# A conformer block on one core: the first chunk of attention scored by seven-product quads, with the key sums computed on GpSimd

## The chip, the cores and the metric

The kernel runs on one core of one Trainium2 chip. The core has a matrix engine (PE in the profile; its weight loads are listed as PEld), a vector engine (DVE), a scalar engine (ACT), GpSimd (POOL) and a queue engine for transfers (SP). Each engine works through its own instructions in order and waits on semaphores for the others. The metric is the device time of one execution in microseconds. Three timed runs of the kernel before the change gave 1851.18, 1851.48 and 1852.26 us, so the median is 1851.48 us.

## The reference

The input is x with 2 batches of 4000 tokens of 512 features, in bf16. Cut to what matters here, the block is:

```
x1 = x + 0.5 * (silu(LN(x) @ w_ff1_a) @ w_ff1_b)
h = LN(x1); q, k, v = h @ w_q, h @ w_k, h @ w_v
p = softmax(q k^T / sqrt(512)); x2 = x1 + (p v) @ w_o
x3 = x2 + conv module (pointwise, gate, depthwise 3, norm over all tokens, silu, pointwise)
x4 = x3 + 0.5 * (silu(LN(x3) @ w_ff2_a) @ w_ff2_b); result LN(x4)
```

The attention is full: each of a batch's 4000 tokens looks at all 4000 tokens. In the kernel w_q and w_k are folded into one matrix M, so the scores are (h M) h^T and the keys are the rows h themselves; w_v and w_o are folded in the same way.

## The kernel before

**Chunks.** The tokens are cut into 16 chunks of up to 512, eight for each batch (the last of a batch has 416). First all chunks pass the first feed-forward part, then `attention` (line 2242) runs over the 16 chunks g as chunks of queries, with the convolution of earlier chunks woven in, and then the second feed-forward part follows. Chunk 0 is the first chunk of the first batch, chunk 8 the first of the second batch.

**Scores.** The keys of a batch are 32 tiles of 128 tokens (tiles 0 to 31; tile 31 is short), and attention steps over them as kt = 0 to 31. A plain tile (`scores`, line 1822) takes four matmuls, one for each 128 of the 512 features, with 512 queries as columns; `exp_pair` takes the exponential out of PSUM. Four tiles can instead be taken together as a quad (`score_quad`, line 2185; quad q holds tiles 4q+2 to 4q+5, and there are seven). A quad sees the keys as a 2x2 matrix of blocks (even and odd tile, lower and upper half of the features) and the queries likewise (halves of the features and of the chunk), and uses Winograd's form of Strassen's product: seven block products instead of eight. Each product is four matmuls of 256 columns. A quad has four steps, at kt = 4q+2 to 4q+5, in three PSUM banks c, x and h. Step 0: product 5 into x, ACT copies it to m5; product 1 into c, ACT copies c to h. Step 1: product 6 onto h, DVE writes x = h + m5, product 2 onto c, exponential of c. Step 2: product 7 onto h, DVE writes m5 = h + m5, product 3 onto x, two exponentials. Step 3: product 4 onto h, exponential of h. `half_quad` does the same for tiles 0 and 1.

**Sums ahead of the products.** The products need sums of blocks. Those of the queries (`q_sums`, line 2086) are four operations for a chunk. Those of the keys (`k_sums`, line 2100) are four operations for a quad on 128x512 bf16: s1 = a21 + a22, s2 = s1 - a11 and s4 = a12 - s2 go to a buffer KF, of which there are two (`k_home` says which of them a quad uses), and a21 is overwritten by a11 - a21. `k_here` issues them in two halves and two ticks later stores the buffer to DRAM (`kfd`); the other chunks of the batch load it again (`k_stream`). All these sums run on DVE.

**Which chunks use quads.** Chunk 0 is plain for tiles 0 to 30, since its key sums are only made in its course, for quad q at kt = 4q+6 and 4q+7 (function `forms`, line 2294), after the plain scores of those tiles. All other chunks use quads. Chunk 8 uses them from the start of its batch: its key sums are made for quads 0 and 1 at the end of chunk 7 and for quads 2 to 6 four ticks ahead of each. Plain scores of chunk 0 rotate through banks 0, 1 and 2, the very banks c, x and h of quads.

**The second product.** p v is taken for pairs of tiles, again by seven products (`pv`), into banks 3 to 6 and so on; its sums of exponentials (`pair_sums`) and of values (`v_here`, in chunk 0) run on DVE.

**What sets the order.** The program only lists operations with the buffers that they read and write. A planner (class `Plan`, line 112) gives each a cost and puts them on the engines in the order in which they would come ready: an engine other than PE may take work up to 16 us ahead of where PE stands in the listed order, and PE may reorder within 8 us (line 2942). Its cost of an operation of n elements is 450 + n ns on POOL (line 148) and 150 + 0.52 n ns for a two-operand bf16 operation on DVE. The order that it finds is fixed in the program; at run time each engine's queue is strictly in order. POOL's queue in chunk 0 also holds a one-column memset behind each load of a tile of values (`key_values`, line 2464), which waits for that load. SP's queue holds all transfers of this stage.

Of the kernel before, what the change touches and what calls it, by code (L numbers as in the profile page):

```python
# [19 lines left out]
TCB = -(-T // CHUNK)  # L20
FC = F // 128
NCK = B * TCB
# [6 lines left out]
QUADS = 7  # L29
HC, HD, HF = CHUNK // 2, D // 2, FC // 2  # L30
KT = -(-T // 128)
# [10 lines left out]
def width(c):  # L42

    return CHUNK if c % TCB < TCB - 1 else T - (TCB - 1) * CHUNK
# [515 lines left out]
class Conformer:  # L560
# [1539 lines left out]
    def k_sums(self, g, q, step):  # L2100

        S, n, b = self.S, self.k_home(g, q), g // TCB
        if step == 4:
            self.k_move(g, q, True)
            return
        if q < 0:
            a11, a12, a21, a22 = [self.hh[:, r, e] for r in range(2) for e in range(2)]
            s1, s2, s4 = [self.KF[n][:, m, 0].rearrange("p j k -> p (j k)") for m in range(3)]
            b_x = self.b_hT[0][0:2]
        else:  # L2110
            x = self.hq[:, q]
            b_x = [self.b_hT[kt // TPC][kt % TPC] for kt in self.quad_tiles(q)]
            a11, a12, a21, a22 = [x[:, :, r, e].rearrange("p u j k -> p u (j k)") for r in range(2) for e in range(2)]
            s1, s2, s4 = [self.KF[n][:, m].rearrange("p u j k -> p u (j k)") for m in range(3)]
        b1, b2, b4 = [[c] for c in self.b_KF[n]]
        out, u, v, op, rd, wr = ((s1, a21, a22, ALU.add, [], b1), (s2, s1, a11, ALU.subtract, b1, b2),
                                 (s4, a12, s2, ALU.subtract, b2, b4), (a21, a11, a21, ALU.subtract, [], b_x[1::2]))[step]
        S.op("DVE", lambda e: e.tensor_tensor(out=out, in0=u, in1=v, op=op), reads=rd + b_x, writes=wr)

    @staticmethod  # L2120
    def k_home(g, q):
        return (q + (g % TCB > 0)) % 2 if q >= 0 else 0

    def k_move(self, g, q, away):

# [116 lines left out]
    def attention(self, old, hook, between):  # L2242

        S = self.S
        for g in range(NCK):
            W, plain = width(g), g == 0
            for kt in range(KT):
                if plain:
                    self.ring = [0, 1, 2]
                else:  # L2250
                    self.ring, self.rings["S"] = list(self.ASIDE.get(kt, (0, 1))), 0
                if 0 < g < NCK - 1 and kt < 2:
                    self.query_quad(g + 1, 1 if kt == 0 else 3)
                if plain and kt < KT - 1 or g % TCB < 1 + (g < TCB) and kt < 2 or kt == KT - 2:
                    ps, b_ps = self.scores(g, kt, None if plain else self.bank(kt if kt < 2 else 0))
                    if kt < KT - 2:
                        self.exp_pair(g, kt, ps, b_ps)
                    else:
                        self.act(self.P30[:, 0:W], ps[:, 0:W], AF.Exp, [b_ps], [self.b_P30], scale=SCALE)
                elif not plain and kt < KT - 2:  # L2260
                    S.front(1000)
                    for step in ((0,), (1, 2), (3,))[kt] if kt < 3 and g % TCB > (g < TCB) else ():
                        self.half_quad(g, step)
                    if kt > 1:
                        self.score_quad(g, *divmod(kt - 2, 4))
                    S.front(0)
                if g < NCK - 2:
                    if kt == KT - 1:
                        self.query_quad(g + 2, 0)
                    if 23 <= kt < 27:  # L2270
                        self.query_sums(g + 2, kt - 23)
                if 0 < g < NCK - 1 and kt == 0:
                    self.query_quad(g + 1, 2)
                if g == 0 and 21 <= kt < 25:
                    self.query_weights(kt - 21)
                if g == 0 and kt < 2:
                    self.pop(old // 2 if kt == 0 else old - old // 2)
                if kt == (21 if g == 0 else 24 if g < NCK - 1 else 16):
                    self.tail_scores(g)
                if g:  # L2280
                    self.units_late(g - 1, kt)
                between(g, kt)
                self.units(g, kt)
                self.next_queries(g, kt, 9 if g else 0)
                hook(g, kt)
                self.forms(g, kt)
                self.keys_swap(g, kt)
                self.tick()
# [5 lines left out]
    def forms(self, g, kt):  # L2294

        if g + 1 < NCK and 27 <= kt < 31:
            self.q_sums(g + 1, kt - 27)
        q, r = divmod(kt - 6, 4)
        if g == 0 and 0 <= q < QUADS and r < 2:
            self.k_here(0, q, r)  # L2300
        for at in {1: (26, 27), TCB: (29, 30)}.get(g, ()):
            if kt == at:
                self.k_here(g, -1, kt % 2 == g % TCB)
        q, r = divmod(kt + 2, 4)
        if r < 2:
            if g == TCB and 1 < q < QUADS:
                self.k_here(g, q, r)
            if g == TCB - 1 and q >= QUADS:
                self.k_here(g + 1, q - QUADS, r)
        q, r = divmod(kt + 3, 4)  # L2310
        if r == 0 and q and (g % TCB if q < QUADS else g and (g + 1) % TCB) and (q != QUADS or g % TCB > (g < TCB)):
            self.k_stream(*((g, q) if q < QUADS else (g + 1, q - QUADS - 1)))
        if g == 0 and kt == 30:
            self.k_stream(1, 0)
        if g:
            if kt == 2:
                self.v_stream(g, 1)
            j, r = divmod(kt + 1, 4)
            if r == 0 and 1 < j < GROUPS:
                self.v_stream(g, j)  # L2320
        if kt == KT - 1 and g + 1 < NCK:
            self.v_stream(g + 1, 0)
# [612 lines left out]
    def program(self, any_score):  # L2935
        i = self.i
        self.any_score = any_score
        S = self.S
# [89 lines left out]
        for dc in range(DC):  # L3028
            self.q_group(0, 0, dc)
            if not any_score:  # L3030
                self.tick()
        if not any_score:
            for n in (0, 1, 2, 3, 4):
                self.v_here(0, n)
        self.pop(1)
# [182 lines left out]
        for k in range(2):  # L3218
# [3 lines left out]
            for ti in pair:  # L3222
# [3 lines left out]
                                                            in1=self.neghalf[0:TILE, two], op=ALU.pow),  # L3226
                 reads=self.b_mv[sl][two] + [self.b_neghalf], writes=self.b_rs[sl][two])
            S.op("DVE", lambda e, two=two: e.scalar_tensor_tensor(
                out=self.sh[sl][:, two], in0=self.mv[sl][:, two, 0], scalar=-1.0, in1=self.rs[sl][:, two],
# [8 lines left out]
        for h in range(2):  # L3238
            for f, (ps, b_ps) in enumerate(self.early):
                out = ps[:, h * HC:(h + 1) * HC].rearrange("p (t k) -> p t k", t=2)  # L3240
# [116 lines left out]
```

## Time and profile before

| what | value |
|---|---|
| median of three runs | 1851.48 us (1851.18 to 1852.26) |
| the profiled execution | 1851.06 us, span of its instructions 1846.9 us |
| granted PE clock | 1.000 |
| busy share of the span | PE 99%, PEld 82%, DVE 81%, ACT 74%, POOL 8% |
| chunk 0 of attention | about 402 to 458 us of the span |
| chunk 8 of attention | about 870 to 932 us of the span |

The profile was taken on a run that is 0.42 us below the median. Its span runs from the first to the last instruction. A row of grouped instructions has the engine, the operation, the regions written and read (out<-in), the shape, the count, then the busy time in us and the mean duration of one in ns, then the idle time of the engine ahead of them and who ended it. The regions are large: "keys" holds key tiles and values, "sums" the exponentials and their sums, "xt" the residual stream and in attention the KF, query-sum and m5 buffers, "work" queries and outputs, "wff" weights and convolution buffers; "s" and "y" are the PSUM banks 0 to 3 and 4 to 7. A row of the timeline has start, length, engine, operation and count, where equal neighbours are merged. A row of a window has its length and for each engine the busy time and the count of instructions.

### The profile page before, as it was taken

The numbers are of one execution on the slowest core, as the hardware profiler recorded it, in microseconds if no ns is written. First come the engines' busy times: TensorE is split into PE (matmuls) and PEld (weight loads), VectorE is DVE, ScalarE is ACT, GpSimd is POOL, SyncE is SP. The second block draws the span as 40 slices with busy tenths as digits, with TensorE's granted clock in tenths as the row PEclk, the third lists the DMA queues.
The fourth block names the chain that finished last, engine by engine and source line by source line (L and its number), as shares of the span: only waits on it lengthen the run. The fifth ranks groups of instructions, "written<-read, shape, count | busy, mean of one in ns | idle before, by whom it ended". The sixth has DMA issues, their size and how long they took to land.

```text
span 1846.9 us, 40836 instructions
## 1 busy us (share of the span) xinstructions
PE 1827.6 (99%) x16082; PEld 1518.8 (82%) x16168; DVE 1491.3 (81%) x3240; ACT 1364.9 (74%) x2433; POOL 144.3 (8%) x357
## 2 busy tenths in 40 slices
PE   9999999999999999999999999999999999999998
PEld 6888888866888888889878888888876888888887
DVE  8889898868766877677876777777779989889886
ACT  6887777755656877787777877887768788777775
POOL 2000000000000000000100000000011000000010
PEclk9999999999999999999999999999999999999999
DMA  7332344287645655458954444543476222211211
GB/s 200 87 91 85 83 111 100 70 245 226 173 144 143 189 153 157 125 151 178 241 146 136 123 116 117 146 122 111 124 218 171 56 69 77 73 47 48 64 44 45
DMA packets 317722, 231.09 MB, mean 125 GB/s; under 512 B 191362, under 2 KB 288325, under 8 KB 317268
## 3 DMA queue, kind: packets, MB, share of 16 engines
q1 hardware_dynamic: 316996, 228.15, 45.7%
q8 instruction: 129, 2.11, 0.5%
q14 instruction: 69, 0.57, 0.1%
q10 hardware_dynamic: 528, 0.26, 0.0%
HBM read 131.15 MB, written 56.22 MB: 101 GB/s over the span
## 4 chain that ended last, share of the span: by engine, by line
PE 95%; DVE 2%; ACT 1%; DMA 1%; issue 1%; SPq 0%; DVEq 0%; ACTq 0%
PE y L95 50%; PE s L95 45%; DVE work L95 1%; ACT work L95 0%; DVE wff L95 0%; ACT sums L95 0%; DMA work<-work 0%; DMA pqd<-wff 0%; ACT keys L95 0%; DVE xt L95 0%; DVE sums L95 0%; DVE s L95 0%; DMA xt<-kfd 0%; DVE keys L95 0%; ACT xt L95 0%
## 5 line engine op out<-in xcount | busy, mean ns | idle before, releaser
L95 ACT ACTIVATE sums<-s 128x512 bf16<-128x512 f32 (+4 forms) x498 | 291.3, 586 | 145.9 <-PE s L95 143.0
L95 ACT ACTIVATE keys<-s 128x512 bf16<-128x512 f32 (+3 forms) x275 | 156.9, 574 | 132.7 <-PE s L95 101.6
L95 DVE TENSOR_TENSOR sums<-sums 128x512 bf16<-128x512 bf16 (+3 forms) x528 | 201.3, 399 | 54.6 <-ACT sums L95 42.2
L95 PE MATMUL y<-work,keys 128*128 128x256 bf16 x1920 | 244.4, 273 | 0.0
L95 PE MATMUL s<-sums 128*128 128x256 bf16 (+1 forms) x1428 | 212.6, 272 | 0.1
L95 PE MATMUL y<-sums,keys 128*128 128x256 bf16 (+1 forms) x1440 | 210.6, 270 | 0.0
L95 PE MATMUL y<-wff,keys 128*128 128x256 bf16 (+2 forms) x1590 | 209.4, 276 | 0.1
L95 ACT ACTIVATE work<-xt,work 128x512 bf16<-128x512 bf16 x260 | 199.5, 784 | 9.5 <-DVE work L95 7.8
L95 PEld LDWEIGHTS y<-work,keys 128*128 128x128 bf16 x1920 | 187.8, 98 | 22.4
L95 PE MATMUL y<-work,wff 128*128 128x256 bf16 (+3 forms) x1324 | 197.2, 272 | 0.1
L95 DVE TENSOR_TENSOR keys<-keys 128x1024 bf16<-128x1024 bf16 (+2 forms) x264 | 170.7, 660 | 22.9 <-ACT keys L95 20.2
L95 PE MATMUL s<-work,keys 128*128 128x256 bf16 (+4 forms) x1329 | 184.6, 275 | 1.0
L95 PEld LDWEIGHTS y<-wff,keys 128*128 128x128 bf16 (+1 forms) x1592 | 151.4, 98 | 30.2 <-issue 3.4
L95 DVE BATCH_NORM_STATS2 work<-xt 128x6 f32<-128x512 bf16 x251 | 164.3, 681 | 2.4 <-DMA xt<-in_x_dram 1.7
L95 PEld LDWEIGHTS s<-sums 128*128 128x128 bf16 x1428 | 139.0, 98 | 22.5 <-DVE s L95 0.4
L95 PEld LDWEIGHTS y<-sums,keys 128*128 128x128 bf16 x1440 | 138.1, 98 | 21.3 <-issue 2.9
L95 POOL TENSOR_TENSOR work<-work 128x4 f32<-128x4 f32 (+3 forms) x108 | 91.2, 845 | 764.8 <-DVE work L95 741.8
L95 PE MATMUL s<-xt,keys 128*128 128x256 bf16 (+1 forms) x924 | 142.3, 270 | 1.2 <-DVE s L95 1.1
L95 PEld LDWEIGHTS y<-work,wff 128*128 128x128 bf16 x1324 | 127.3, 98 | 17.6 <-DVE wff L95 0.4
L95 PE MATMUL y<-sums,xt 128*128 128x256 bf16 (+1 forms) x960 | 140.7, 270 | 0.3 <-DVE sums L95 0.3
L95 PEld LDWEIGHTS s<-work,keys 128*128 128x128 bf16 (+1 forms) x1348 | 107.7, 97 | 34.9 <-ACT sums L95 2.2
L95 PE MATMUL s<-xt 128*128 128x256 bf16 (+1 forms) x893 | 131.4, 270 | 1.3 <-DMA xt<-kfd 0.9
(163 smaller groups left out, 3343.9 us busy)
## 6 DMA issues: line engine op xcount, KB each, us to landing
xt<-kfd SPq DMA_DIRECT2D x98, 384.0 KB, 3.2
xt<-v12d SPq DMA_DIRECT2D x105, 256.0 KB, 3.1
xd<-xt SPq DMA_DIRECT2D x28, 512.0 KB, 2.7
xt<-xd SPq DMA_DIRECT2D x28, 512.0 KB, 3.8
out_dram<-xt SPq DMA_DIRECT2D x14, 512.0 KB, 2.9
xt<-in_x_dram SPq DMA_DIRECT2D x13, 512.0 KB, 4.4
dcvd<-wff SPq DMA_DIRECT2D x48, 128.0 KB, 2.9
keys<-dcvd SPq DMA_DIRECT2D x12, 512.0 KB, 3.7
```

The source lines that it names most:

```text
L95: return getattr(eng, self.name)(*self.args, **self.kw)
```

## The change

Chunk 0 is plain only for kt below 6 and for tile 30. Its tiles 6 to 29 are scored as quads 1 to 6. For that, `q_sums` of chunk 0 (four operations on DVE) are issued right after its queries, and the key sums of quads 1 to 6 are issued ahead of the quads: of quad 1 at kt = 0 and 1, of quad 2 at 3 and 4, of quad q from 3 to 6 at 4q-3 and 4q-2. Quad 0's key sums follow at kt = 25 and 26, in the other of the two KF buffers than before, in which chunk 1 finds them without a load; the load at kt = 30 is gone. The scores of the short last tile move from kt = 21 to 24 in chunk 0, and scores in chunk 0 from kt = 6 take the banks that they take in other chunks (this also holds for the four groups of chunk 1's queries at kt = 16, 17 and 20). All key sums, of both batches and also those of tiles 0 and 1, are issued on POOL instead of DVE.

```diff
@@ k_sums
-        S.op("DVE", lambda e: e.tensor_tensor(out=out, in0=u, in1=v, op=op), reads=rd + b_x, writes=wr)
+        S.op("POOL", lambda e: e.tensor_tensor(out=out, in0=u, in1=v, op=op), reads=rd + b_x, writes=wr)
@@ k_home
-        return (q + (g % TCB > 0)) % 2 if q >= 0 else 0
+        return (q + (g % TCB > 0 or g + q == 0)) % 2 if q >= 0 else 0
@@ attention
-            W, plain = width(g), g == 0
+            W = width(g)
             for kt in range(KT):
+                plain = g == 0 and kt < 6
...
-                if plain and kt < KT - 1 or g % TCB < 1 + (g < TCB) and kt < 2 or kt == KT - 2:
+                if plain or g % TCB < 1 + (g < TCB) and kt < 2 or kt == KT - 2:
...
-                if kt == (21 if g == 0 else 24 if g < NCK - 1 else 16):
+                if kt == (24 if g < NCK - 1 else 16):
                     self.tail_scores(g)
@@ forms
-        q, r = divmod(kt - 6, 4)
-        if g == 0 and 0 <= q < QUADS and r < 2:
-            self.k_here(0, q, r)
+        if g == 0:
+            q, r = (1, kt) if kt < 2 else (2, kt - 3) if kt < 7 else divmod(kt + 3, 4)
+            if 0 <= r < 2 and q <= QUADS:
+                self.k_here(0, q % QUADS, r)
...
-        if g == 0 and kt == 30:
-            self.k_stream(1, 0)
@@ program
         if not any_score:
+            for n in range(4):
+                self.q_sums(0, n)
             for n in (0, 1, 2, 3, 4):
                 self.v_here(0, n)
```

## The prediction

> **What bounds the kernel now.** I read the page's busy shares first, then its chain that ended last, then windows over the two stretches that the change touches, with the neighbours of chunk 0 as a measure.
>
> ```profile
> span 1846.9 us, 40836 instructions
> PE 1827.6 (99%) x16082; PEld 1518.8 (82%) x16168; DVE 1491.3 (81%) x3240; ACT 1364.9 (74%) x2433; POOL 144.3 (8%) x357
> PE 95%; DVE 2%; ACT 1%; DMA 1%; issue 1%; SPq 0%; DVEq 0%; ACTq 0%
> core 0: us, PE busy (x) PEld busy (x) DVE busy (x) ACT busy (x) POOL busy (x), PEclk, DMA share, GB/s
> 402.00:458.00 56.00, 55.74 (x347) 32.92 (x351) 37.41 (x101) 29.98 (x50) 3.28 (x26) 1.00 0.79 246
> 458.00:518.00 60.00, 59.79 (x534) 49.20 (x538) 43.81 (x103) 37.92 (x71) 2.54 (x9) 1.00 0.66 173
> 518.00:580.00 62.00, 61.08 (x552) 51.43 (x555) 43.48 (x102) 39.69 (x76) 2.70 (x12) 1.00 0.55 152
> 870.00:932.00 62.00, 60.91 (x562) 51.02 (x564) 53.86 (x130) 48.41 (x90) 4.63 (x15) 1.00 0.98 235
> ```
>
> PE is busy for 99% of the span, PE is 95% of the chain, and the clock is full. In chunk 0 (402 to 458 us) PE idles 0.26 us in 56. The end is therefore set by how many columns PE streams. A saved column is saved time, and anything that lets PE wait is lost time. In chunk 8 (870 to 932), which already works by quads with their key sums on DVE, DVE is busy 53.86 of 62 us (87%), and PE idles 1.09 us: that is what quads cost beside a crowded DVE.
>
> **The change part by part. Columns of PE.** Busy time can't price a matmul, since neighbours overlap, so I take runs of equal matmuls in the timeline, and the mean of one from the groups by shape.
>
> ```profile
> 411.93 5.34 PE L95 MATMUL s<-work,keys 128*128 128x512 bf16 x24
> 585.08 1.25 PE L95 MATMUL y<-sums,keys 128*128 128x256 bf16 x10
> 586.83 1.04 PE L95 MATMUL s<-work,xt 128*128 128x256 bf16 x8
> L95 PE MATMUL s<-work,keys 128*128 128x512 bf16 x173 | 43.5, 379 | 1.0
> L95 PE MATMUL s<-work,xt 128*128 128x256 bf16 x438 | 65.0, 273 | 0.0
> ```
>
> A run of n lasts n-1 steps and one full matmul. With 512 columns the step is (5.34 - 0.379) / 23 = 0.2157 us; with 256 columns (1.25 - 0.273) / 9 = 0.1086 and (1.04 - 0.273) / 7 = 0.1096, so 0.109. Four plain tiles are 16 x 0.2157 = 3.451 us, a quad is 28 x 0.109 = 3.052. Six quads save 6 x 0.399 = 2.4 us. The weight loads grow from 16 to 28 for four tiles; chunks that are all quads have PEld at 82% (49.20 of 60) with PE full, so that costs nothing.
>
> **What the quads add on ACT and DVE, and what DVE loses.**
>
> ```profile
> L95 ACT ACTIVATE s<-s 128x512 f32<-128x512 f32 x103 | 60.3, 585 | 19.4 <-PE s L95 16.6 <-PE y L95 2.0
> L95 ACT ACTIVATE xt<-s 128x512 f32<-128x512 f32 x103 | 61.2, 595 | 28.8 <-PE s L95 27.7
> L95 ACT ACTIVATE sums<-s 128x512 bf16<-128x512 f32 x329 | 195.6, 596 | 127.2 <-PE s L95 125.6
> L95 DVE TENSOR_TENSOR s<-s,xt 128x512 f32<-128x512 f32 x103 | 71.9, 698 | 53.3 <-PE s L95 47.8 <-ACT xt L95 3.9 <-PE y L95 0.2
> L95 DVE TENSOR_TENSOR xt<-s,xt 128x512 f32<-128x512 f32 x91 | 62.5, 686 | 26.4 <-PE s L95 26.3
> L95 DVE TENSOR_TENSOR xt<-xt,keys 128x512 bf16<-128x512 bf16 x14 | 5.9, 420 | 0.3
> L95 POOL TENSOR_TENSOR wff<-wff 128x512 bf16<-128x512 bf16 x2 | 2.3, 1156 | 9.5 <-ACT wff L95 9.5
> ```
>
> The exponentials stay as many (four for four tiles, 128x512 each, 0.60 us). ACT gets two copies for each quad, 12 x 0.59 = 7.1 us, and stands at 29.98 + 7.1 = 37 of some 54 us. DVE gets two additions for each quad, 6 x (0.698 + 0.686) = 8.3 us, and four query sums, 4 x 0.42 = 1.7. It loses 28 key sums (7 quads x 4; the row x14 is s2 alone, 7 quads of 2 batches), 28 x 0.42 = 11.8. That leaves 37.41 + 8.3 + 1.7 - 11.8 = 35.6 us. POOL gets 28 x 1.156 = 32.4 us in chunk 0. In chunks 7 and 8 DVE loses 11.8 us and POOL gets the same 32.4; the few sums of tiles 0 and 1 are half as wide, four for each batch, and go with them.
>
> **GpSimd beside DVE.** POOL has so far almost nothing to do in attention, so what it takes from DVE has to be read elsewhere. Early in the program four GpSimd operations on 128x512 run beside DVE:
>
> ```profile
> 23.91 1.28 DVE L95 TENSOR_TENSOR work<-wff 128x1024 bf16<-128x1024 bf16 x2
> 24.75 7.60 POOL L95 TENSOR_SCALAR keys<-keys,work 128x512 bf16<-128x512 bf16 x4
> 25.23 1.79 DVE L95 TENSOR_TENSOR work<-work,wff 128x1024 bf16<-128x1024 bf16 x2
> 28.47 1.78 DVE L95 TENSOR_TENSOR keys<-keys 128x1024 bf16<-128x1024 bf16 x2
> 30.51 1.24 DVE L95 TENSOR_TENSOR sums<-sums,wff 128x512 bf16<-128x512 bf16 x2
> 31.67 0.68 DVE L95 TENSOR_TENSOR sums<-s,sums 128x512 f32<-128x512 f32 x1
> ...
> 1380.38 1.16 POOL L95 TENSOR_TENSOR wff<-wff 128x512 bf16<-128x512 bf16 x1
> 1380.68 1.05 DVE L95 TENSOR_SCALAR work<-xt,work 128x512 bf16<-128x512 bf16 x1
> L95 DVE TENSOR_SCALAR work<-xt,work 128x512 bf16<-128x512 bf16 x18 | 7.2, 437 | 0.1
> ```
>
> Two DVE operations that take 1.28 us alone take 1.79 and 1.78 beside POOL, and two of 0.42 take 1.24: 0.51 + 0.50 + 0.40 = 1.4 us over four POOL operations, 0.35 for each. The nearest row of POOL's own two-operand form held another kind of DVE operation for 1.05 - 0.44 = 0.61 us. So the bounds for one key sum on POOL are 0 (DVE is just then at an addition that reads PSUM, as the 0.68 at 31.67, which is not longer) and 1.156 (DVE stands for all of it). I take 0.35, since those rows are DVE's two-operand sums, what it does most here. Then DVE in chunk 0 is at 35.6 + 28 x 0.35 = 45.4 of 53.6 us, 85%, and in chunk 8 at 53.86 - 11.8 + 9.8 = 51.9 of 62, 84%: relieved there by 2 us only. Beside a DVE at 87% PE idled 1.09 us in chunk 8, so I give chunk 0 after the change 0.9 us of PE idle where it has 0.26: 0.65 us lost. For chunk 8 I take no change, with bounds of -1.1 us (its idle goes) and +1.1 (it doubles).
>
> The Trainium skill, in "SBUF — State Buffer", section "Who interferes with whom", says that a DVE instruction with two SBUF inputs contends with a GpSimd instruction that reads SBUF, and that the later of the two stands still until the first is through. The trace agrees that they hold each other up, but by 0.35 us for a POOL operation of 1.9, not by all of it. By the page's rule the sum would turn to the first rival below.
>
> **The queues.** POOL's longest key sums depend on one another (s1, s2, s4), so a quad takes about 4 x 1.2 to 1.5 = 5 to 6 us there. Six quads fill the time after the plain tiles, some 37 us (the plain run in the timeline ends at 411.93 + 5.34 = 417.3, chunk 0 would end near 455), 6.2 us for each. A KF buffer is free again after product 3, two thirds through its quad, and is needed filled one quad and a third later, some 8 us. So POOL keeps up, with 2 us to spare, and the planner, which counts 962 ns for such an operation where the trace has 1156, is off by less than that. The sums of quads 1 and 2 depend on nothing late and may go up to 16 us ahead. What they can get behind on POOL is this:
>
> ```profile
> POOL keys L95 <- DMA keys<-keysd: 20.1, 18, 6.3
> PE s L95 <- DMA xt<-kfd: 0.9, 1, 0.9
> L95 POOL MEMSET keys<- 128x1 bf16 x24 | 2.2, 100 | 21.9 <-DMA keys<-keysd 20.1 <-DMA keys<-tailsd 1.8
> ```
>
> In chunk 0 POOL waits 18 times for a load of values, up to 6.3 us; a key sum listed behind such a memset waits too, and with it its quad. In turn the memsets now come up to 1.2 us later behind a sum; the values of tiles 15 and up are used ten ticks later, so that is hidden. On SP, the stores of KF wait for POOL where they waited for DVE, and loads queue behind them. One load of 384 KB (quad 0 for chunk 1) goes. I cost these at nothing, with the memsets as the case in which the cover is gone (rival 3). The moved tail scores and the query groups in banks 0 and 1 lie between quads and add no column.
>
> **Sum.** -2.4 (columns) + 0.65 (idle in chunk 0) + 0 (chunk 8) = -1.7 us. Against the profiled execution that is 1851.06 - 1.7 = 1849.4; the median of the runs is 0.42 above it, so 1849.8 us.
>
> **The rivals.**
> 1. *Slower: POOL and DVE shut each other out.* If each of the 28 POOL sums excludes DVE's two-operand sums for its full length, it holds one up by half of it on the mean, 0.58 us. DVE then needs 35.6 + 16.2 = 51.8 us, and with the 87% that chunk 8 shows as workable chunk 0 lasts 59.5 us instead of 56: 1851.5 + 3.5 = 1855. If chunk 8 suffers too (53.86 - 11.8 + 16.2 = 58.3, at 87% 67 us instead of 62), 1860. For it: the 0.61 us under POOL's two-operand form. Against it: the four sums at 24.75 cost 0.35 each. It decides from about 0.55 us for each sum.
> 2. *The chain of a quad sets the pace.* Bank h passes from copy to product 6, addition, product 7, addition, product 4 and exponential before the next quad may copy into it: 0.59 + 0.6 + 0.70 + 0.6 + 0.69 + 0.6 + 0.6 = 4.4 us (a product is three steps of 0.109 and one matmul of 0.273), with some 0.07 at each of seven hand-overs 4.9. In other chunks 62 / 8 = 7.75 us are there for four tiles, here 6.2. If queueing on ACT and DVE adds 2 us, six quads take 41.4 instead of 37.2: +4.2 - 2.4 = +1.8, so 1853.3.
> 3. *The sums come late.* One quad held for the 6.3 us of the longest load wait gives -2.4 + 6.3 = +3.9, so 1855.4. Against it: the planner may place sums of quads 1 and 2 16 us ahead of that wait.
> 4. *More than the columns.* If chunk 8's 1.09 us of idle also goes and chunk 0 gets none, -2.4 - 1.1 = -3.5; with a further stall gone by a new order (0.9 for the load of KF is the longest kind beside) 1847.2.
>
> **How the numbers follow.** A measurement of this kernel can tell about 0.2%, 3.7 us, from no change, so below 1847.8 is faster and above 1855.2 slower. Chances: the forecast (1848.2 to 1850.9) 0.58; rival 1 0.14; rival 2 0.15 (1851 to 1855); rival 3 0.04; rival 4 0.09. Faster is most of rival 4, 0.07; slower is rival 1 and part of 2 and 3, 0.17; within it 0.76. The likeliest is 1849.8. The range from 1847.6 to 1854.6 leaves out the bottom of rival 4 (some 0.05) and rival 1 with most of rival 3 (some 0.15).
>
> **What would show it.** Plain groups of 512 columns in chunk 0 fall from 120 matmuls by 96, and 168 of 256 columns come. POOL shows 56 operations of 128x512, near 1.16 to 1.5 us. DVE's two-operand sums in chunk 0 have a tail of 0.75 to 0.9 us. PE's idle in chunk 0 stays under 1.5 us, and the stretch to the end of chunk 0 is about 1.7 us shorter. I am wrong if PE waits there for "DVE s" or "DVE sums" by several us, if PE waits for POOL at all, or if another stage moves by more than 1 us through a new order.

## The result and the profile after

The changed kernel takes 1874.95 us (median of four runs, 1873.42 to 1878.26) against 1851.87 us for the kernel before on the same chip (four runs, 1851.18 to 1853.21): a ratio of 1.0125, 95% interval 1.0112 to 1.0137. It is slower by 23 us. The forecast was 1849.8 us, and the time lies above the range and above the price of every rival.

The profiled execution of the changed kernel took 1873.42 us. Its page begins with the busy shares, and the chain's first row follows:

```profile
span 1869.5 us, 41150 instructions
PE 1833.9 (98%) x16240; PEld 1524.4 (82%) x16240; DVE 1514.0 (81%) x3192; ACT 1372.4 (73%) x2445; POOL 218.4 (12%) x421
PE 91%; DVE 5%; DMA 2%; ACT 1%; issue 1%; SPq 0%; POOL 0%; DVEq 0%; POOLq 0%; ACTq 0%
```

PE's part of the chain falls from 95% to 91% and DVE's rises from 2% to 5%. One number is odd: DVE has 48 instructions fewer than before (3192 for 3240), since the key sums are gone from it, and yet it is busy for 22.7 us more (1514.0 for 1491.3).

The windows of the changed kernel over the stretches that the prediction used for chunks 0 and 8 show where the time goes (same columns as there):

```profile
402.00:458.00 56.00, 46.40 (x344) 30.80 (x343) 45.74 (x85) 30.71 (x52) 25.54 (x47) 1.00 0.77 223
870.00:932.00 62.00, 57.96 (x558) 48.81 (x556) 50.99 (x101) 45.94 (x89) 28.43 (x33) 1.00 0.89 202
```

In 56 us of chunk 0 PE idles 9.6 us where it idled 0.26. DVE is busy for 45.74 us, almost the 45.4 that was forecast, but it got through only 85 instructions, 0.54 us each, where it had 101 of 0.37 us. It is not that DVE has more to do: it does less in more time.

A stage's place can be compared between kernels by when the first ACT copy of a chunk's second-product result (sums<-y) starts. Against the kernel before, this copy is late by the following, in the profiled executions (one each, good to 1 or 2 us; "all sums on DVE" and "second batch alone" are experiments told below; the profiled execution of "all sums on DVE" is the fastest of its ten, 3.2 us under their median, so its column is low):

| at this copy of | changed kernel | all sums on DVE | second batch alone on GpSimd |
|---|---|---|---|
| chunk 2 | +13.5 | +0.8 | +0.7 |
| chunk 6 | +15.7 | +2.1 | +1.3 |
| chunk 9 | +23.3 | +2.3 | +9.5 |
| end of the span | +22.6 | +0.9 | +9.5 |

The loss is made in two places, some 13 us in and right behind chunk 0 and some 7 to 8 us about chunk 8: the two stretches in which GpSimd makes key sums. The largest of PE's waits over the whole changed kernel (engine, line waited for: us in total, times, longest):

```profile
PE s L95 <- DVE s L95: 7.4, 8, 1.4
PE y L95 <- DVE xt L95: 5.5, 2, 3.2
PE s L95 <- DVE sums L95: 4.6, 3, 1.9
```

In the kernel before, the same view has

```profile
PE s L95 <- DVE s L95: 1.1, 2, 0.8
PE y L95 <- DVE xt L95: 0.9, 1, 0.9
PE s L95 <- DVE sums L95: 0.5, 1, 0.5
```

PE waits for DVE and, in the whole trace, not once for POOL. So the key sums are in time (rival 3 is out), and something makes DVE late. The timeline of the changed kernel shows what. First a quad in chunk 0, then the longest stall, at its end (the rows of DVE and GpSimd, and in the last row PE):

```profile
422.15 0.68 DVE L95 TENSOR_TENSOR xt<-s,xt 128x512 f32<-128x512 f32 x1
422.39 1.16 POOL L95 TENSOR_TENSOR xt<-keys,xt 128x512 bf16<-128x512 bf16 x1 [0.78 <-PE s L95]
422.75 1.08 DVE L95 TENSOR_TENSOR xt<-keys,xt 128x512 bf16<-128x512 bf16 x1
423.63 1.22 POOL L95 TENSOR_TENSOR keys<-keys 128x512 bf16<-128x512 bf16 x1
423.87 1.26 DVE L95 TENSOR_TENSOR keys<-keys 128x512 bf16<-128x512 bf16 x1
...
458.03 1.42 POOL L95 TENSOR_TENSOR xt<-xt,keys 128x512 bf16<-128x512 bf16 x1
458.36 4.29 DVE L95 TENSOR_TENSOR sums<-sums 128x512 bf16<-128x512 bf16 x4
459.58 1.16 POOL L95 TENSOR_TENSOR xt<-keys,xt 128x512 bf16<-128x512 bf16 x1
460.82 1.21 POOL L95 TENSOR_TENSOR keys<-keys 128x512 bf16<-128x512 bf16 x1
462.57 0.41 DVE L95 TENSOR_TENSOR xt<-work 128x512 bf16<-128x512 bf16 x1
462.91 0.41 DVE L95 TENSOR_TENSOR xt<-keys 128x512 bf16<-128x512 bf16 x1
463.35 0.43 DVE L95 TENSOR_TENSOR xt<-keys,xt 128x512 bf16<-128x512 bf16 x1
...
463.83 1.03 PE L95 MATMUL y<-sums,xt 128*128 128x256 bf16 x4 [3.24 <-DVE xt L95]
```

In the kernel before, four such sums in a row read

```profile
416.28 1.68 DVE L95 TENSOR_TENSOR sums<-sums 128x512 bf16<-128x512 bf16 x4 [0.27 <-ACT sums L95]
```

A two-operand sum on DVE that meets a key sum on GpSimd takes 1.26 us instead of 0.42 and ends about when GpSimd's ends (423.87 + 1.26 = 425.13, beside 423.63 + 1.22 = 424.85). The trace gives starts and ends alone, so whether DVE stands or only crawls meanwhile is not told apart. Four in a row beside three key sums take 4.29 us instead of 1.68. What DVE has behind them, here a sum of values that PE needs for the second product, comes later, and PE stands for 3.24 us. The addition at 422.15, which reads PSUM and one operand of SBUF, takes its usual 0.68 us beside a key sum.

### The profile page after: what moved, and what is told of

It is laid out like the page before. It is cut to its first block, busy times and chain, and to the rows that moved or that the text cites. A ratio compares the mean times of both kernels' runs of the same rounds, so it can differ in the third digit from the quotient of the medians.

```text
span 1869.5 us, 41150 instructions
## 1 busy us (share of the span) xinstructions
PE 1833.9 (98%) x16240; PEld 1524.4 (82%) x16240; DVE 1514.0 (81%) x3192; ACT 1372.4 (73%) x2445; POOL 218.4 (12%) x421
## 4 chain that ended last, share of the span: by engine, by line
PE 91%; DVE 5%; DMA 2%; ACT 1%; issue 1%; SPq 0%; POOL 0%; DVEq 0%; POOLq 0%; ACTq 0%
PE y L95 49%; PE s L95 42%; DVE sums L95 2%; DVE work L95 1%; DVE xt L95 1%; DVE wff L95 0%; ACT work L95 0%; DMA dcvd<-wff 0%; DMA work<-work 0%; ACT sums L95 0%; DMA wff<-in_w_ff_a_dram 0%; DVE s L95 0%; DMA xt<-v12d 0%; DMA wff<-keysd 0%; DVE keys L95 0%
## 5 line engine op out<-in xcount | busy, mean ns | idle before, releaser
L95 DVE TENSOR_TENSOR sums<-sums 128x512 bf16<-128x512 bf16 (+3 forms) x528 | 221.0, 436 | 56.4 <-ACT sums L95 44.2
L95 PE MATMUL y<-wff,keys 128*128 128x256 bf16 (+3 forms) x1592 | 210.0, 276 | 0.0
L95 DVE TENSOR_TENSOR keys<-keys 128x1024 bf16<-128x1024 bf16 (+2 forms) x248 | 166.4, 685 | 23.0 <-ACT keys L95 20.2
L95 PE MATMUL s<-work,keys 128*128 128x256 bf16 (+4 forms) x1300 | 172.4, 269 | 4.1 <-DVE xt L95 2.4
L95 PEld LDWEIGHTS s<-sums 128*128 128x128 bf16 x1428 | 139.0, 98 | 22.6 <-DVE s L95 0.4
L95 PE MATMUL s<-xt,keys 128*128 128x256 bf16 (+1 forms) x972 | 149.9, 271 | 7.6 <-DVE s L95 7.4
L95 PE MATMUL s<-xt 128*128 128x256 bf16 (+1 forms) x941 | 138.6, 270 | 1.4 <-ACT s L95 1.1
L95 DVE TENSOR_TENSOR s<-s,xt 128x512 f32<-128x512 f32 (+1 forms) x125 | 85.6, 685 | 63.5 <-PE s L95 52.7
```

What stands on the lines that cost most here:

```text
L95: return getattr(eng, self.name)(*self.args, **self.kw)
```

## The experiments

Theory A: while GpSimd makes a two-operand sum, DVE's two-operand sums on SBUF stand still; DVE works strictly in order, so the whole queue behind is late, and PE with it. Theory B: the quads are too tight a chain for chunk 0 (rival 2). Theory C: the key sums or the order that the planner finds are at fault, not the engine; the texts on record call the planner's part of it Theory D. Each ratio below is against the kernel before on the same chip.

### The key sums back on DVE, the quads kept

```diff
@@ k_sums (the changed kernel)
-        S.op("POOL", lambda e: e.tensor_tensor(...
+        S.op("DVE", lambda e: e.tensor_tensor(...
-        WEIGHTS, TOKENS, TAPS = (14, 16, 18, 20), (24, 25, 26, 27), (8, 11, 14, 17)
+        WEIGHTS, TOKENS, TAPS = (27, 28, 29, 30), (24, 25, 26, 27), (8, 11, 14, 17)
```

The second edit makes the convolution's weight sums later, behind the key norm that reads the same memory; the third run of this list shows what it does alone.

> The changed kernel with all key sums back on DVE (the four sums of the convolution's weights are listed at kt = 27 to 30 instead of 14 to 20, so that they stay behind the norm that still reads the same memory). Theory A, exclusion: while POOL works on a two-operand sum no two-operand sum of DVE starts, and that is the whole loss. Then the loss goes: DVE in chunk 0 is at about 47 of 54 us, PE idles about 1 us there, 1849 to 1853 us. Theory B, the quads of chunk 0 follow one another too tightly (their chain of copies and additions sets the pace): 1862 to 1868 us, with chunk 0 as long as in the changed kernel and only chunk 8 better.

Measured: 1855.18 us (ten runs), ratio 1.0013 (1.0003 to 1.0022). That is above the 1849 to 1853 us expected by theory A and far below theory B's 1862 to 1868. The window and PE's waits of 402 to 458 us:

```profile
402.00:458.00 56.00, 52.75 (x403) 36.84 (x405) 42.18 (x109) 36.19 (x62) 4.04 (x30) 1.00 0.85 245
...
PE s L95 <- ACT s L95: 1.3, 2, 0.8
PE y L95 <- DVE xt L95: 0.8, 1, 0.8
PE s L95 <- DVE s L95: 0.4, 1, 0.4
```

With the key sums back, DVE does 109 instructions in 42.18 us, and 21 of the 23 us are gone. So the loss needs the key sums on GpSimd, and the quads alone do not make it. But the quads bring nothing either: PE now idles 3.25 us in chunk 0, in waits of under 1 us each for ACT's copies (1.3 us), for a sum of values by DVE (0.8) and for DVE's additions (0.4), and that eats the 2.4 us of saved columns. The stalls lie at 435 to 452 us, while quads 1 to 3 (415 to 431 us) run without one.

### The key sums on GpSimd, without quads in chunk 0

```diff
@@ k_sums (the kernel before)
-        S.op("DVE", lambda e: e.tensor_tensor(...
+        S.op("POOL", lambda e: e.tensor_tensor(...
```

> The kernel before with all key sums on POOL and nothing else changed: chunk 0 stays plain. Theory A: DVE's two-operand sums beside POOL's take up to 1.26 us instead of 0.42 in both batches; chunk 8 loses its 6 us as in the changed kernel, chunk 0 loses less than 14 since no quad waits for DVE there: 1858 to 1866 us. Theory B: chunk 0 has no quads, so nothing is lost there, and chunk 8 loses at most what late sums cost: 1851 to 1854 us.

Measured: 1868.64 us (four runs, 1866.99 to 1871.18), ratio 1.0078 (1.0061 to 1.0095).

```profile
402.00:458.00 56.00, 50.86 (x290) 27.34 (x294) 40.23 (x65) 26.91 (x45) 32.04 (x52) 0.97 0.73 226
```

Chunk 0 has no chain of a quad here, and still PE idles 5.1 us in these 56, while DVE does 65 instructions in 40.23 us, 0.62 each. At chunk 2's copy this kernel is 11.8 us late, the changed kernel 13.5. Theory B can't be the cause of that.

The profile is of the slowest of the four executions, 2.5 us above their median. By the medians the size does depend on the quads: without them in chunk 0, the key sums on GpSimd cost 0.78%, with them 1.17% (1.013 of the next run less the 1.0013 above), and the difference of some 7 us is larger than the intervals allow for noise. So about two thirds of the loss need no quad in chunk 0. That the tighter chain of a quad makes the same hold dearer would fit the rest, and no run here shows it. Theory A had expected 1858 to 1866 us, and the time is above that too.

### The changed kernel with the weight sums late

The second edit of the first experiment alone.

> The changed kernel with the four sums of the convolution's weights listed at kt = 27 to 30, the second difference that the run with all sums on DVE had. Both theories: this does not matter, 1873 to 1878 us as the changed kernel. If it gained more than 5 us, part of what was put down to POOL would belong to these sums.

Measured: 1876.45 us (two runs), ratio 1.013 (1.011 to 1.0151), where the changed kernel has 1.0125. The edit does not explain what the key sums on DVE gave back.

### Idle sums on GpSimd that nobody waits for

In the kernel before, GpSimd adds two constant tiles into a tile that nobody reads at that time, once for each key tile of the first 26 of chunk 0. No key sum and no quad is touched, and DVE and ACT run the same operations in the same order as before.

```diff
+                if g == 0 and 0 <= kt < 26:
+                    out = self.QF[3].rearrange("p j k -> p (j k)")
+                    S.op("POOL", lambda e: e.tensor_tensor(out=out, in0=self.Wvo[:, 0, :], in1=self.Wvo[:, 1, :], op=ALU.add), ...
```

> The kernel before with 26 more operations on POOL in chunk 0, one for each kt, that add two 128x512 bf16 pieces of a weight into memory that nobody reads: no one waits for them. Theory A: some 20 of DVE's two-operand sums grow to 0.8 to 1.26 us, DVE's busy time in chunk 0 grows by 8 to 15 us, and the time by 2 to 8 us although nothing depends on POOL. Theory B, and the theory that the sums come too late: no change, 1851 to 1853 us, and DVE's sums stay at 0.42.

Measured: 1859.98 us (seven runs), ratio 1.0036 (1.0025 to 1.0047). First the busy shares of the page (DVE had 1491.3 us for the same 3240 instructions before), then the window, then lines of the timeline:

```profile
PE 1831.8 (99%) x16082; PEld 1519.3 (82%) x16168; DVE 1510.8 (81%) x3240; ACT 1364.6 (73%) x2433; POOL 175.1 (9%) x383
402.00:458.00 56.00, 50.52 (x289) 27.32 (x293) 48.61 (x94) 27.08 (x45) 28.75 (x50) 0.97 0.73 224
...
436.42 3.00 DVE L95 TENSOR_TENSOR sums<-sums 128x512 bf16<-128x512 bf16 x3
436.56 2.58 POOL L95 TENSOR_TENSOR xt<-work 128x512 bf16<-128x512 bf16 x2
438.18 0.61 PE L95 MATMUL s<-sums,keys 128*128 128x256 bf16 x4 [1.58 <-DVE sums L95]
```

Work that no one needs costs 6.7 us (0.36%). DVE's busy time over the whole span rises by 19.5 us (1510.8 - 1491.3) for the same instructions, which is 0.75 us for each of the 26 idle sums. In the window alone it rises by 11.2 us (48.61 - 37.41), but only 21 of the 26 lie in it, and DVE gets seven instructions less done there. Three sums of 0.42 us take 3.00 us beside two on GpSimd. This is theory A by itself: the engines' meeting, not the lateness of anything GpSimd makes, and not a new order.

### The same with copies: one operand read

```diff
+                    S.op("POOL", lambda e: e.tensor_copy(out, self.Wvo[:, 0, :]), ...
```

> As the run with 26 idle two-operand operations, but with copies on POOL, which read one operand. If each operation of POOL that reads shuts DVE's two-operand sums out for its whole length, they grow by up to the length of the copy; if it is the second operand of POOL that collides, they stay near 0.42 to 0.8 and the time near 1852 us.

Measured: 1852.7 us (eight runs), ratio 0.9999 (0.9989 to 1.001). The busy shares, the group of the copies, the window, and two lines of the timeline:

```profile
PE 1826.7 (99%) x16082; PEld 1518.9 (82%) x16168; DVE 1496.9 (81%) x3240; ACT 1365.9 (74%) x2433; POOL 162.4 (9%) x383
L95 POOL COPY xt<-work 128x512 bf16<-128x512 bf16 x26 | 18.2, 700 | 0.8
402.00:458.00 56.00, 55.72 (x348) 32.85 (x352) 41.86 (x104) 31.08 (x53) 15.17 (x48) 1.00 0.81 248
403.57 0.69 POOL L95 COPY xt<-work 128x512 bf16<-128x512 bf16 x1
403.82 0.71 DVE L95 TENSOR_TENSOR xt<-keys,xt 128x512 bf16<-128x512 bf16 x1
```

A sum on DVE that meets a copy takes 0.71 instead of 0.42 us. DVE's busy time rises by 5.6 us over the span (1496.9 - 1491.3), 0.22 for each copy, and the time does not move: PE idles 0.28 us in the window, where it idled 0.26.

### The same with writes: no operand read

Two constants written (memset) for each of the 26 tiles, 52 in all.

```diff
+                    for _ in range(2):
+                        S.op("POOL", lambda e: e.memset(out, 0.0), ...
```

> The kernel before with 52 writes of a constant by GpSimd (128x512, bf16) into a tile that nobody reads at that time, two for each key tile of the first 26 of chunk 0. It asks whether it is reading that holds VectorE off. If only operands that are read count: VectorE's two-operand sums beside them stay at 0.42 us each, its busy time from 402 to 458 us stays at about 37.4 us, and the time is that of before, 1852 to 1854 us. If a write holds it off as well: busy time up by 0.1 us or more for each, 5 us or more in all, and the time 1 to 5 us above that of before, as with e3.

Measured: 1852.4 us (eight runs) against 1851.62, ratio 1.0002 (0.9992 to 1.0013). The busy shares, the group, the window, and two lines of the timeline:

```profile
PE 1831.8 (99%) x16168; PEld 1519.8 (82%) x16168; DVE 1492.6 (81%) x3240; ACT 1365.1 (74%) x2433; POOL 170.1 (9%) x409
L95 POOL MEMSET xt<- 128x512 bf16 x52 | 27.2, 524 | 2.2
402.00:458.00 56.00, 56.00 (x354) 33.12 (x353) 37.44 (x101) 29.88 (x50) 20.66 (x62) 1.00 0.80 249
427.74 1.22 DVE L95 TENSOR_TENSOR sums<-sums 128x512 bf16<-128x512 bf16 x3
427.84 2.85 POOL L95 MEMSET xt<- 128x512 bf16 x5
```

GpSimd is busy for 20.66 us of the window, and DVE's 101 instructions take 37.44 us, as before (37.41); over the span DVE's busy time is 1.3 us up for 52 writes. Three sums beside five writes take 1.22 us, 0.41 each. Here and with the copies, too, DVE and ACT keep the order of the kernel before. So it is what GpSimd reads that holds DVE's sums off.

### A quarter of the sums on GpSimd

In the changed kernel only the fourth sum of each four (a11 - a21, on which no other sum of its quad waits) stays on GpSimd; the weight sums are late.

```diff
-        S.op("POOL", lambda e: e.tensor_tensor(...
+        S.op("POOL" if step == 3 else "DVE", lambda e: e.tensor_tensor(...
```

> The changed kernel with one sum of four on POOL (a21, which no other sum waits for) and three on DVE; convolution weights late. Theory A, exclusion for the length of each POOL sum: a quarter of the POOL sums, so a quarter of the 20 us between the changed kernel and the one with all sums on DVE, ratio 1.003 to 1.005, and DVE's sums that meet one still take up to 1.26 us. Theory C, the loss comes from the three dependent sums s1, s2, s4 being late on POOL: they are on DVE here, so the ratio is that of all sums on DVE, 1.001.

Measured: 1860.61 us (four runs), ratio 1.0047 (1.0031 to 1.0064). Above the kernel with all sums on DVE (1.0013) that is 0.34%, for a quarter of the sums, where all of them cost 1.17% (1.013 less 1.0013). A quarter of that would be 0.29%, so within the intervals a quarter of the sums, spread over both batches, makes a quarter of the loss, and it does so without the chain of dependent sums, which is on DVE here. The loss does not go by the count alone: the next run has twice as many sums on GpSimd, all in the second batch, and loses no more.

### Key sums of the second batch alone on GpSimd

```diff
-        S.op("POOL", lambda e: e.tensor_tensor(...
+        S.op("DVE" if g < TCB else "POOL", lambda e: e.tensor_tensor(...
```

> The changed kernel, its key sums of the first batch (chunk 0) by VectorE, those of the second batch (chunk 8) by GpSimd, and the convolution's weight sums late as in e1. Exclusion (a two-operand sum on GpSimd holds off VectorE's two-operand sums while it runs): chunk 0 goes as in e1 and loses nothing, chunk 8 loses the 6 to 7 us that the joins of the changed kernel show for it; time 1859 to 1863 us against about 1853 before, a ratio of 1.003 to 1.006. If the loss needs the quads' chains as well as GpSimd's sums (a sum that comes late for a chain that cannot wait), chunk 8 is as in the changed kernel too, since its quads are the same in both; if on the other hand chunk 8's loss is only chunk 0's carried on, the time is that of e1, 1854 to 1856 us.

Measured: 1860.61 us (four runs, 1859.75 to 1862.45) against 1851.62, ratio 1.0048 (1.0031 to 1.0064).

```profile
402.00:458.00 56.00, 52.97 (x408) 36.91 (x407) 42.27 (x108) 36.32 (x62) 4.12 (x30) 1.00 0.85 250
870.00:932.00 62.00, 55.85 (x509) 46.02 (x508) 50.11 (x95) 42.38 (x80) 32.98 (x38) 0.98 0.95 219
```

Chunk 0 is that of the kernel with all sums on DVE (52.97 for 52.75 of PE). Chunk 8, which was already made of quads in the kernel before, loses: PE idles 6.2 us where it idled 1.09. Above the kernel with all sums on DVE the time is 0.35%, 6.5 us; from chunk 6 to chunk 9 the table of single profiles has 7.6 us for the changed kernel and 8.2 for this one. The second batch loses on its own, and the first batch is left with the larger part.

### The planner's price of a key sum

The planner counts 962 ns for such an operation on GpSimd. Here it counts 1500.

```diff
-            return 1000 if call.name == "tensor_tensor" and n < 8 else 450 + n
+            return 1000 if call.name == "tensor_tensor" and n < 8 else 1500 if call.name == "tensor_tensor" and n == 512 else 450 + n
```

> The changed kernel with the planner's price for a 512-element two-operand operation on POOL set to 1500 ns instead of 962, so that it lists engines' work for POOL sums as slow as the trace shows or slower. Theory D, the plan is wrong about POOL's speed and all engines run in an order made for faster sums: at least half of the loss goes, 1853 to 1863 us. Theory A: the planner still does not know that DVE stands still, 1868 to 1880 us.

Measured: 1879.52 us (two runs), ratio 1.0147 (1.0127 to 1.0167): no better than the changed kernel. An order that knows GpSimd to be slow does not help, since the plan still doesn't know that DVE stands meanwhile. This part of theory C falls; an order that keeps DVE's sums and GpSimd's apart was not tried.

### The queries of chunk 1 ahead

The stalls that the quads leave on DVE lie among the four groups of chunk 1's queries, which since the change take the banks that other chunks use. Here, with all sums on DVE, they come at kt = 6 in a row.

```diff
-            plan = {14: (0,), 16: (1,), 18: (2,), 20: (3,)} if self.any_score else {16: (0,), 17: (1, 2), 20: (3,)}
+            plan = {14: (0,), 16: (1,), 18: (2,), 20: (3,)} if self.any_score else {6: (0, 1, 2, 3)}
```

> Quads in chunk 0 with all sums on DVE, and chunk 1's four query groups listed at kt = 6 in banks 3, 5 and 7, which are empty until then, instead of at 16, 17 and 20 in banks 0 and 1, which the quads use. Theory B for what is left of the loss (the quads' banks and chain): PE's idle of 3 us in chunk 0 falls under 1.5, and the time falls by 1.5 to 3 us against the run with query groups in banks 0 and 1, to a little below the kernel before (ratio 0.998 to 1.000). If the rest was DVE's load (42 of 56 us), nothing changes: ratio 1.001.

Measured: 1853.74 us (ten runs), ratio 1.0006 (0.9997 to 1.0016).

```profile
402.00:458.00 56.00, 53.17 (x409) 37.28 (x411) 42.06 (x108) 34.62 (x60) 3.65 (x26) 1.00 0.88 244
```

PE's idle in chunk 0 goes from 3.25 to 2.83 us, and the stalls move to 417 to 419 and 438 to 442 us. That the query groups cause them is not borne out. This is the best of the kernels with the quads, and it can't be told from the kernel before.

## Why the prediction was wrong

**The columns.** The matmuls changed as foretold (the count of weight loads rises by 72, from 16168 to 16240, which is 168 - 96), and nothing contradicts the 2.4 us. But they were not time. With the key sums on DVE the quads make the kernel 0.13% (0.03 to 0.22%) slower, 2.4 us, where columns and idle were to give -1.7. The idle of chunk 0 was taken as 0.9 us and is 3.25, in waits for ACT's copies and for DVE. This is rival 2 in its size (it had +1.8) and in the engines that PE waits for; that it is the length of a quad's chain was not shown, and the stalls lie in one part of chunk 0 only. What makes them there stays open.

**GpSimd beside DVE: the step that failed.** "I take 0.35, since those rows are DVE's two-operand sums, what it does most here." The rows were of the right operation on DVE and of the wrong one on GpSimd, a TENSOR_SCALAR. The runs show that GpSimd's side decides: for each idle operation on the mean, DVE lost next to nothing beside a write, 0.22 us beside a copy, and 0.75 us beside a two-operand sum (0.84 in the pair shown above). In the changed kernel GpSimd makes 56 key sums of 128x512 and eight of half that width. By my count in its timeline, DVE's two-operand sums on 128x512 last 21.7 us longer there than at 0.42 us each, and its other shapes some 11.6 us longer, so 33 us in all and 0.5 to 0.6 us for each key sum, within the bounds of 0 and 1.156 and on the mark from which rival 1 was to decide. The sign that was named for being wrong came: PE waits for "DVE s" and "DVE sums" 12.0 us in all, where it waited 1.6. The nearest row of GpSimd's own two-operand form (0.61 us) was quoted, and set aside for four rows of another form.

```profile
L95 DVE TENSOR_TENSOR sums<-sums 128x512 bf16<-128x512 bf16 x408 | 181.4, 460 | 48.7 <-ACT sums L95 38.6
L95 POOL TENSOR_TENSOR xt<-keys,xt 128x512 bf16<-128x512 bf16 x14 | 17.8, 1268 | 12.8 <-PE s L95 11.8
L95 POOL TENSOR_TENSOR keys<-keys 128x512 bf16<-128x512 bf16 x14 | 17.4, 1240 | 1.0
```

In these groups of the changed kernel, DVE's sums of exponentials have a mean of 460 ns. The first of them reads in the kernel before:

```profile
L95 DVE TENSOR_TENSOR sums<-sums 128x512 bf16<-128x512 bf16 x408 | 165.5, 422 | 49.1 <-ACT sums L95 38.8 <-DVE sums L95 0.5
```

GpSimd's key sums are held up too, from the 1156 ns of the row in the prediction to 1240 and 1268.

**From DVE's load to the time.** The second fault is in the forecast and in rival 1 alike, and it is why even that rival, with 0.58 us for each sum, was priced at 1855 to 1860 and not at 1875. Both turned the hold into a load of DVE and read from chunk 8 what PE idles beside such a load: the forecast had 0.9 us for a busy time of 45.4 us, and the runs have 9.6 us of idle at 45.74, a load met by luck, since DVE got less done in it. Load is not what counts. In the kernel with idle sums, DVE is busy 48.61 of 56 us, 87%, the very share of chunk 8 in the kernel before, and PE idles 5.5 us where chunk 8 has 1.09. With the key sums on GpSimd and no quads, DVE is busy only 40.23 us, 72%, and PE idles 5.1. With copies DVE is at 41.86 us, 75%, and the time rose by nothing. What differs in these runs is the length of one delay. My reading, which no run tests by itself, is that a hold of 0.3 us is taken up by the slack between DVE and PE, while holds of 0.84 us in a row make an in-order queue 2.6 us late (4.29 less 1.68), and PE stands.

**A clock that falls.** No step had this. Behind the longest stall of the changed kernel the granted clock goes down for some microseconds:

```profile
460.00:464.00 4.00, 0.76 (x7) 0.42 (x5) 3.83 (x7) 0.60 (x1) 1.95 (x2) 0.89 0.00 0
464.00:468.00 4.00, 4.00 (x27) 3.05 (x26) 2.72 (x7) 0.69 (x2) 0.11 (x1) 0.68 0.56 164
```

From 460 to 464 us PE works 0.76 us, and from 464 to 468 it gets through 27 matmuls at a clock of 0.68. In the kernel before, the same four microseconds hold 39 matmuls at 1.00; 12 more steps of 0.109 us are 1.3 us, an estimate of what it cost. The kernel with idle sums shows the same behind a stall of 2.67 us that begins at 420.21 us (a clock of 0.60 from 424 to 428 us), while behind one of 2.22 us, at 448.84 us of the changed kernel, the clock was 1.00 from 452 to 456 us. So a part of what the holds cost in these runs is the clock's.

**Chunk 8** was costed at no change, with bounds of 1.1 us either way. It loses 6.5 us by the medians (second batch alone). That GpSimd takes 11.8 us of work from DVE there is no relief: the window of the changed kernel has DVE at 50.99 us for 101 instructions, where it was 53.86 for 130.

**What held.** The queues: PE never waits for GpSimd, and a higher price in the plan does not help. The additions that read PSUM are not held (0.68 us beside a key sum). The Trainium skill, "SBUF — State Buffer", section "Who interferes with whom", says that a DVE instruction with two SBUF inputs contends with a GpSimd instruction that reads SBUF and not with one that only writes it. The trace agrees with both halves: 1.26 us beside a sum that reads, 0.41 beside a write. That the later of the two stands until the first is through, as the prediction took it from there, is nearly so for two-operand sums (0.84 of 1.2 us in the pair shown) and less so for copies (0.29 of 0.70 us in the pair shown). The section says this in so many words of DVE's two-port modes, not of a sum with two inputs. The rule that was weighed and set aside was the better guide to the cost of one sum, though not to the time.

**The sum, rebuilt.** The quads with all sums on DVE +2.4 us (0.13%); the second batch's sums on GpSimd +6.5 (0.35%); the rest, of the first batch's, 23.1 - 2.4 - 6.5 = 14.2, for which the table shows 13.5 - 0.8 = 12.7 by chunk 2. These parts leave some 1.5 us to the uncertainty of single profiles. The 14.2 us are what is left over and not a price of the sums by themselves: without quads, the first batch's sums cost some 8 us by the medians (0.78% less 0.35%).

## What to carry to other kernels

Work moved from DVE to GpSimd does not leave DVE free: when both read SBUF with two operands, DVE's sum hardly gets on while GpSimd's runs, and GpSimd's is the longer (1.16 for 0.42 us), so the move costs DVE at least as much as the sum that it gave away (0.5 to 0.75 us here). Price an overlap by rows in which both engines have the forms in question, and weigh the longest delay in an in-order queue, not the sum of busy time. Idle work on the suspected engine, which no one waits for, tells such a conflict from a late result in one run.

## What was not expected of the hardware

DVE's loss beside GpSimd goes by what GpSimd reads: 1.3 us in all for 52 writes of 0.524 us, 0.22 us for each of 26 copies of 0.70 us, 0.75 us for each of 26 two-operand sums of 1.2 us. And a stall of 3.24 us on PE is paid twice: the clock behind it was 0.68 over the next 4 us, and 0.57 in the same four microseconds of the kernel with GpSimd's sums and no quads, which had worked 0.74 us of the four before them:

```profile
460.00:464.00 4.00, 0.74 (x7) 0.68 (x8) 3.89 (x7) 0.60 (x1) 1.52 (x2) 1.00 0.08 28
464.00:468.00 4.00, 4.00 (x24) 2.94 (x23) 3.77 (x11) 0.24 (x1) 0.00 (x0) 0.57 0.67 198
```
